# A gated mix of an S4 convolution and linear attention on one core: the written-out issue order, the engine of each step, the PSUM rings and the per-unit forms replaced

## The chip, the cores and the metric

The kernel runs on one core of one Trainium2 chip. The metric is the device time of one execution in microseconds (us); lower is better. The core has five engines that run side by side, each in its own program order: PE (matrix multiply), DVE (vector), ACT (activation functions and copies), POOL (general) and SP (which only issues DMAs here).

## The reference, cut to what matters

Input is one sequence x of 2048 tokens by 512 channels. Two branches are computed from it and mixed by a gate.

```python
g = sigmoid((x * gate_w).sum(-1))
# a: S4 convolution. K[d, l] = Re sum_n C[d,n] * exp(dt*A[d,n]*l) * dt*B[d,n]   (N = 128 states)
#    y = causal convolution of x with K along the tokens (an FFT in the reference), + x * Dskip
# b: linear attention, 32 heads of 16
pq, pk = q @ w_phi, k @ w_phi
phi = concat(softmax(p), softmax(-p))          # for q and for k
kv, z = phi_k^T v, phi_k summed over tokens
o = (phi_q @ kv) / (phi_q @ z + 1e-6);  b = o @ wo
out = g * a + (1 - g) * b
```

Complex exponentials come out as Sin on ACT times Exp on ACT; the softmaxes take Exp on ACT, and their divisions are done as Exp of minus Ln, also on ACT.

## The kernel before, in words

The kernel is built in two passes. First it makes a list of 1058 *nodes*, small steps with a name, an engine, dependencies and a function that issues the step's instructions. Then `Plan.run` goes through the nodes in the order of a string, ORDER (two base-64 digits for a node), and issues each. Since each engine works in program order, the string fixes every engine's sequence; semaphores between engines follow from the dependencies. Further strings fix the rest: SIDES says on which of two engines a step with a choice runs (mostly PSUM evictions, on ACT or DVE), RINGS from which pool of PSUM a step takes its tile, FOURS and ZPS which of two forms some units take. WARM is all zeros.

The steps that matter here, with numbers in the order of their making (`rz#3` is the fourth `rz`):

- Head: `par`, `ld`, `ud`, `wsm`, `wqk`, `wv` are loads on SP's queue; `tgs` (Sin) and `tga` (Abs) make the FFT's tables; `p_e`, `p_d`, `p_g`, `p_ce` (Exp), `p_ab` (Abs) and `p_sn` (Sin) make the tables of the convolution's kernel; `xT` and `udc` bring x into place; `wTe` and `wpe` evict the folded weights.
- FFT of x: matmuls `psAu` and `psBu`, evictions `XAu` and `XU`, 16 each.
- Attention keys, eight pairs of token tiles: `pk` (PE), `ek` (Exp, twice), `zp` (PE) and `zk` (DVE) sum the softmax, `rz` (Ln, then Exp on ACT) inverts the sum, `vp` (PE) and `vb` (eviction) make v, `vr` (DVE) scales it, `kn` (PE) accumulates. ZPS has a digit for each pair: 1 sums groups of four on PE with eight matmuls by the identity and leaves DVE one reduction (L739); 0 lets DVE do it all with two reductions (L736).
- Attention queries, four blocks of 512 tokens: `pq`, `eq` (Exp), `zs`, `z1` (Ln, Exp), `z2`, `z3` (Ln), `z4`, `z5` (Exp), a round trip by DMA, `em`, `ops`, `oT`, `bpsq`, `bs3`. The last block's steps end in L (`eqL`, `z1L`, ...).
- Convolution kernel, 16 units of 32 channels: `argC` (PE) and `cs` (Sin, twice), `argE` (PE) and `E` (Exp), `El`, `Rh`, `Rl`, `A1`, `A2`, `A3` (DVE), `kps` (PE, L183), `KD` (eviction). FOURS has a digit for each unit: 0 adds two products on DVE (`A3`, L1110) and runs 64 matmuls; 1 leaves the add out and runs 128 matmuls.
- FFT of K, product with that of x, and back: `psA`, `XA`, `psB`, `XK`, `t`, `psz`, `Zr` or `Zn`, DMAs `zw` and `zr` through DRAM, `psy`, `ou`, and the output DMAs `out` and `outL` on SP's or ACT's queue. `Y` and `bsg` evict parts of the sum.

ACT holds one table of functions at a time. Nodes `tabT` and `tabL` (the table `natural_log_exp_and_others`) load one explicitly, five times each, through `Tables.begin` (L65); all functions are issued through `Tables.__call__` (L68). Copies and Abs are made from either table. In the list of nodes, each node says which table it wants (`tab=`) and which node sets it (`sets=`), but only the head's Sin and Exp nodes are tied to the table's node by a dependency ("act"), besides the `cs` nodes, which stand in phases between a `tabT` (in the first phase, the end of the head) and a `tabL`; nothing in `run` checks the table.

Of the kernel before, what the change touches and what calls it, by code (L numbers as in the profile page):

```python
# [70 lines left out]
class Plan:  # L71

    DIGITS = "0123456789abcdefghijklmnopqrstuvwxyzABCDEFGHIJKLMNOPQRSTUVWXYZ-_"
    ORDER = ("040B0H0K0d0y0C0D0L0s0I070J0M0P0g000S110j0N08010z0T0m0Q0e2R0a0p0q0r0_0W2T100U0O0V14120Y2U2x0A2S050k130Z2y2V2X2Z0R190v0t0u"
             "0b0c0w2_0l0E0X2W1516172L1a061b2Y022-30311y33340n030f0-"
             "0h1e1f0i1w2J18321c0F0o2B2K2M1n1z1H1g1A1o2D2C1d1p1I091x1E1J351Q1R2F1B0x1C2E0G2H1q36372G2I2P382N2Q391F3b2O3c4C1S3a4J4L4K4M"
             "3d3e4Q4R3f4U1Y3g4N1r4O1h4V3h1L4Y4-"
             "4P3i4Z4_3j4W4S53542z57504T3k4X1Z515b5d58521s1D593l5c3n5i5e55565j3m5a1G3o5q5f5g5s5r5t3p3r3q1T5m5n5u3s5v5h5o5k5w5x5B1P4D4E"
             "3w2v5l5p4F5y5F5C3y1U5H3x5G5I5J5z5A1V5D5E3t3z5U3D5K5V5M5N3A3R3E2w3F5W5L1O5_3G5O5Q5X5Y5Z3B3C1W605R5S1N3K3M1K3S1M5-"
             "5P3L634G642A615T653N673T6869626a666m6n6o3U6p3V3W3X3Y6b6c6q6d6r6s1t3Z3H3-1X3_3O1i1j41401_4221431-"  # L80
             "1k1l204445466e272923222b282d4748243P491m2a4a2c2e4b4g2f4c2g4d252h2o4e4h4i4n1u4j3u3v2j4p2i2l2k2m2q2p6i262s4q4o1v4k2n4u2r2t"
             "6f4v4w6j4r3I2u4x4y4z6g4l8l3J4A8p8m6t6u6k6v8q3Q4f4s6x6h8k8o6l8n8r8s6y6z6w6A6C4m4t4B8C6G8t6I6K8w8x8y8u6B6H6J4H8D8v6L6M6N7d"
             "8z8A8E4I8B7e7f8I7g8F6F9e8Q8G8H9b6O6P8R7h7j7i6Q6R8J9f7M7N8S6S6T6U6Vaeaf7O8W8X8K7k9g8L8T8U8Z8-"
             "938M8N7l6D8_7m8V7n6W6X6Y8O8P8Y7P94an7o7pao7q6_70717r90917Qa47S9295ag7R6Z7s6-"
             "72aha8a9966Ea7akaca5ai73aa75979998ajap7677a69aalatamab74ad7TaBaC7t797u7v7U78au7y7z7V7w7x9caq9naras7AavaH7W9d9h9o9paw7X9v"
             "aY9waK7Y7ZaDaL9q9raZ7a9x9y9zaIc57B7-aM9kc69D9EaQaEbX9L7Cb_aF7D9M7_9Ac07EaRaG9iaxaz80ay9B818285bYaA7Ga-"
             "7IaJ86879j9Fc19s7Jb-"
             "9l9m9Na_7bc7aNaOaPc3cbb2b37HbZc283aS9C7FaT849G9H9I9t89aUaWaV8baX7cccc8c99O9u9P9Q9R888cb87Kb9b0c4caceb19J8abacfcgbg8dck9K"
             "8ecl8f8gbbbh8hbcbibob4cP9Sbpbqcd9T8ichci7L8jcBcCcjcsdYcYctcucycDczdZd-cQcR9Ucmd_cHcvcw9W9Xcnbj9VbwbkblbxcocIbre0eLcp9Ze1"
             "e2b5b6eMbse3eUeVcxb7bye4cqbtbu9Ybdbe9-"  # L90
             "9_cAcrcSbme5cZdOdScEbfcFcGcTcUe6a0a1bve7dTdRdWeNa2e8cJcKe9bzbAedeecLeRcNcOa3eSeaebeOcMc_ePbBd0ecd1d7cVd8d9cWeCdfcXeWdPdU"
             "d2daefege-e_eQd3dbdQdgeTdVd4dndodXdhdcg1g2dieDeEdjeXbKfAbCbnbDbEbFeYfBeZf0f1bGc-dpbLddg7dqbHd5f2drbMf3f4f5bNfGbIbJbOezdk"
             "eAfDdsfEeBeIf6f7feffdldtbPdebQdBfCfHehdueifFejdmf8fgeJd6ekdvfIfJdyf9fafhfbg4fifKg5g6dwfjdzfkfcdxdCdEfLdAdFfMg3g8dGg9dHfN"
             "fleFelfdfmfpdDdLgagbgcgddIeGemeKfqeHfOfPfQfRgeenepfneofreqeresgfggghgifSfTfUfofsbRgjbSgkdJftetglfVfYfZgmgngobUbVgqfufWdM"
             "dNbWgpf-fvfxfygreufwevewexbTeydKfzfXf_g0gvgwgsgtgugx")
    SIDES = ("011111010010101011001110110010011001010100001011100000000000011000011001111101000100000100000000000000000000000010000000"
             "00100001000000000000000101010000000000000100001101001")
    RINGS = ("001010111111010010100000000000000000000000100000000000000000001101100000000101101011100100100001101010111100111001010100"
             "01111")
    WARM = ("000000000000000000000000000000000000000000000000000000000000000000000000000000000000000000000000000000000000000000000000"  # L100
            "000000000000000000000")
    FOURS = ("0111100101011000")
    ZPS = ("01000111")

    HOT = ("pk", "vp", "pq", "zp", "ops", "bps4", "psA", "psBu", "psB128", "psB64", "psB32", "psz", "pszn", "psyn32", "psy128", "psy64", "psy32", "kps")

# [46 lines left out]
    def run(self):  # L153
        code = {d: i for i, d in enumerate(self.DIGITS)}
        order = [64 * code[a] + code[b] for a, b in zip(self.ORDER[0::2], self.ORDER[1::2])] or list(range(len(self.nodes)))
        assert sorted(order) == list(range(len(self.nodes)))
        sides, rings, warm = iter(self.SIDES), iter(self.RINGS), iter(self.WARM)
        for n in self.nodes:
# [501 lines left out]
def attention_keys(P, nc, g, psum, r):  # L660
# [40 lines left out]
    for s2 in range(8):  # L701
# [20 lines left out]

        def ps4(K=K, box=box, on=P.ZPS[s2] == "1"):
            if not on:
                return
            box.ps = bank("zk")
            for u in range(2):
                e = K.E[:, u].rearrange("p g (h a b) -> p (g h) a b", a=4, b=4)
                for k in range(4):
                    nc.tensor.matmul(box.ps[:, 256 * u:256 * u + 256], lhsT=g.ident[:], rhs=e[:, :, k, :], start=(k == 0), stop=(k == 3), skip_group_check=True)  # L730

        def rd(K=K, box=box, on=P.ZPS[s2] == "1"):
            K.Z = g.kwk.tile([128, 2, 2, 32], F32, name="Zk")
            if not on:
                for u in range(2):
                    nc.vector.tensor_reduce(out=K.Z[:, u].rearrange("p g h -> p (g h)"), in_=K.E[:, u].rearrange("p g (h f) -> p (g h) f", f=16),  # L736
                                            axis=mybir.AxisListType.X, op=ALU.add)
                return
            nc.vector.tensor_reduce(out=K.Z[:].rearrange("p u g h -> p (u g h)"), in_=box.ps[:].rearrange("p (z b) -> p z b", b=4), axis=mybir.AxisListType.X, op=ALU.add)  # L739
            box.ps = None  # L740
# [294 lines left out]
def plan_exp(P, nc, g, psum, U, T, psq, deps):  # L1035

    act = g.act
    h, cc = U // 2, U % 2
    box = Bag()

    def pe():
        T.E = g.epool.tile([128, 2, 32, 32], BF16, name="E", bufs=g.P.k["E"])
        box.ps = psum([128, 2, 16, 32], "args")
        for e in range(2):
            nc.tensor.matmul(box.ps[:, e], lhsT=g.statE[64 * e:64 * e + 64, h, :], rhs=g.selE[64 * e:64 * e + 64, 16 * cc:16 * cc + 16, :],
                             start=True, stop=True, tile_position=(64 * e, 0))

    def ex():
        act(out=T.E[:, 1], in_=box.ps[:].rearrange("p e x t -> p (e x) t"), func=ACT.Exp)
        box.ps = None  # L1050

    def el():
        nc.vector.tensor_tensor(out=T.E[:, 0].rearrange("p c (t k) -> p c t k", k=2), in0=T.E[:, 1].rearrange("p c (t k) -> p c t k", k=2),
                                in1=g.G[:, 32 * U:32 * U + 32].unsqueeze(2).to_broadcast([128, 32, 16, 2]), op=ALU.mult)
    a = P.add("PE", "argE", pe, deps, take=[psq, "E"], rw=("stE selE", ""))
    T.nE.append(P.add("ACT", "E", ex, [a], drop=["psum"], tab="L"))
    T.nE.append(P.add("DVE", "El", el, T.nE[-1:], rw=("G", "")))

def plan_conv(P, nc, g, psum, r):  # L1060
# [27 lines left out]
    def kgen(units, XA, new, split=False):  # L1088
        K = Bag()
        K.done, kps, nu = [], [], len(units)  # L1090
        for cc, U in enumerate(units):
            t = T[U]
            plan_exp(P, nc, g, psum, U, t, psq, [sh])
            four = P.FOURS[U] == "1"
            c = Bag()
# [530 lines left out]
```

## Time and profile before

| | us |
|---|---|
| median of 3 runs | 266.88 |
| lowest and highest | 266.54, 267.56 |
| profiled execution, first to last instruction | 265.4 |
| PE busy | 208.8 (79%) |
| PE weight loads busy | 144.6 (54%) |
| DVE busy | 233.9 (88%) |
| ACT busy | 221.7 (84%) |
| POOL busy | 8.4 (3%) |
| mean granted PE clock | 0.933 |

The profile gives the execution's own time as its span alone, 265.4 us; the runs' median is 1.5 us above it. Busy time is the time with an instruction under way; ACT and DVE overlap neighbouring instructions by about a tenth of a microsecond, so a sum of lengths is a little above the time taken. A stage is a stretch of the span, in microseconds from its start.

### The profile page before, as it was taken

The numbers are of one execution on the slowest core, as the hardware profiler recorded it, in microseconds if no ns is written. First come the engines' busy times: TensorE is split into PE (matmuls) and PEld (weight loads), VectorE is DVE, ScalarE is ACT, GpSimd is POOL, SyncE is SP. The second block draws the span as 40 slices with busy tenths as digits, with TensorE's granted clock in tenths as the row PEclk, the third lists the DMA queues.
The fourth block names the chain that finished last, engine by engine and source line by source line (L and its number), as shares of the span: only waits on it lengthen the run. The fifth ranks groups of instructions, "written<-read, shape, count | busy, mean of one in ns | idle before, by whom it ended". The sixth has DMA issues, their size and how long they took to land.

```text
span 265.4 us, 10071 instructions
## 1 busy us (share of the span) xinstructions
PE 208.8 (79%) x4512; PEld 144.6 (54%) x4512; DVE 233.9 (88%) x315; ACT 221.7 (84%) x305; POOL 8.4 (3%) x21
## 2 busy tenths in 40 slices
PE   0768899999964678898857648999997598999760
PEld 0657556655653424447536336775786167965450
DVE  6798898989799989999999999999999798997630
ACT  6989599899899998989999999999999698763300
POOL 4700000000000000000000000000000000000000
PEclk9986799999997579999999999999999799999985
DMA  7799100155510687203243366239753499898776
GB/s 195 130 198 231 23 0 6 63 155 161 145 39 2 195 243 196 84 4 112 73 158 84 100 233 203 76 119 196 160 176 119 167 227 201 207 173 184 161 115 99
DMA packets 67547, 35.93 MB, mean 135 GB/s; under 512 B 46000, under 2 KB 62000, under 8 KB 67504
## 3 DMA queue, kind: packets, MB, share of 16 engines
q1 hardware_dynamic: 65648, 34.76, 53.4%
q8 instruction: 35, 0.57, 1.0%
q10 hardware_dynamic: 1856, 0.52, 1.0%
q14 instruction: 8, 0.07, 0.1%
HBM read 22.17 MB, written 13.11 MB: 133 GB/s over the span
## 4 chain that ended last, share of the span: by engine, by line
PE 39%; DVE 30%; ACT 11%; DMA 9%; issue 7%; SPq 1%; DVEq 0%; ACTq 0%
PE pk L709 6%; PE vp L757 5%; DVE A L1100 4%; DVE R L1121 3%; DVE R L1117 3%; DVE A L1105 3%; DVE Eq L913 3%; PE kps L183 3%; DMA ZT<-Zd 3%; PE psy L824 3%; DMA wqk<-in_B_wqkv_dram 2%; ACT xst L149 2%; DMA ax<-apd 2%; ACT trg L68 2%; PE psA L591 2%
## 5 line engine op out<-in xcount | busy, mean ns | idle before, releaser
L68 ACT ACTIVATE cs<-args 128x1024 bf16<-128x1024 f32 x32 | 30.9, 1052 | 0.9 <-PE args L1023 0.9
L183 PEld LDWEIGHTS <-A 128*32 128x32 bf16 x1536 | 26.4, 161 | 4.8 <-issue 2.0
L183 PE MATMUL kps<-R,A 128*32 128x64 bf16 x1536 | 27.9, 229 | 1.1 <-DVE R L1121 0.7
L1263 PE MATMUL psz<-t,TI 128*128 128x512 bf16 x60 | 16.7, 412 | 5.4 <-DVE t L1231 4.1
L1121 DVE TENSOR_TENSOR R<-E,cs 128x2048 bf16<-128x2048 bf16 x16 | 19.6, 1222 | 0.1
L1105 DVE TENSOR_TENSOR A<-Ctab,Dtab 128x2048 bf16<-128x2048 bf16 x16 | 19.6, 1223 | 0.0
L1100 DVE TENSOR_TENSOR A<-Ctab,Dtab 128x2048 bf16<-128x2048 bf16 x16 | 19.6, 1222 | 0.0
L1117 DVE TENSOR_TENSOR R<-E,cs 128x2048 bf16<-128x2048 bf16 x16 | 19.5, 1220 | 0.0
L149 ACT CAST Zr<-psz 128x1024 bf16<-128x1024 f32 x15 | 15.2, 1022 | 5.1 <-PE psz L1263 3.6
L68 ACT ACTIVATE Ek<-pk 128x512 bf16<-128x512 f32 x32 | 16.7, 601 | 3.2 <-PE pk L709 3.0
L757 PE MATMUL vp<-WW,xT 128*128 128x512 bf16 x64 | 17.8, 419 | 0.0
L1231 DVE TENSOR_TENSOR t<-XUX,XK 128x2048 bf16<-128x2048 bf16 x14 | 16.8, 1222 | 0.4 <-ACT XK L149 0.4
L68 ACT ACTIVATE E<-args 128x1024 bf16<-128x1024 f32 x16 | 16.4, 1036 | 0.6 <-DVE R L1121 0.5
L68 ACT ACTIVATE Eq<-pq 128x512 bf16<-128x512 f32 (+1 forms) x28 | 16.6, 687 | 0.2
L149 ACT CAST XA<-psA 128x1024 bf16<-128x1024 f32 (+1 forms) x15 | 14.6, 1007 | 2.7 <-PE psA L190 2.7
L616 PE MATMUL psB<-XAu,TB 64*128 64x128 bf16 x256 | 11.7, 249 | 6.3 <-ACT XAu L149 3.1
L709 PE MATMUL pk<-WW,xT 128*128 128x512 bf16 x64 | 16.4, 396 | 0.0
L149 ACT CAST XK<-psB 128x1024 bf16<-128x1024 f32 (+1 forms) x14 | 13.7, 990 | 2.5 <-DVE XK L151 1.3
L843 PE MATMUL pq<-xT,Wqp 128*128 128x512 bf16 x64 | 15.5, 380 | 0.2 <-ACT xT L149 0.2
L616 PEld LDWEIGHTS <-TB 64*128 64x128 bf16 x256 | 9.5, 110 | 10.0 <-issue 9.9
L190 PE MATMUL psA<-W,KD 128*64 128x128 bf16 x256 | 9.8, 221 | 5.0 <-ACT cs L68 2.9
L65 ACT ACT_TABLE_LOAD x10 | 12.8, 1283 | 0.1
(211 smaller groups left out, 506.9 us busy)
## 6 DMA issues: line engine op xcount, KB each, us to landing
XUX<-XUd SPq DMA_DIRECT2D x32, 256.0 KB
XUd<-xst SPq DMA_DIRECT2D x8, 512.0 KB
ax<-apd SPq DMA_DIRECT2D x16, 256.0 KB
Zd<-Zr SPq DMA_DIRECT2D x15, 256.0 KB
ZT<-Zd SPq DMA_DIRECT2D x6, 512.0 KB
UD<-in_A_u_dram SPq DMA_DIRECT2D x16, 128.0 KB
XUd<-xst SPq DMA_DIRECT2D x8, 256.0 KB
wqk<-in_B_wqkv_dram SPq DMA_DIRECT2D x1, 1024.0 KB
```

The source lines that it names most:

```text
L68: return self.nc.scalar.activation(**kw)
L149: self.nc.scalar.copy(out=o, in_=i)
L183: nc.tensor.matmul(kps[32 * dj:32 * dj + 32, g4, e, :], lhsT=A[:, ka, :, :, d].rearrange("p a b -> p (a b)"), rhs=R[:, kr, d, :], start=(i ...
L616: nc.tensor.matmul(box.ps[:, c2, sl, :], lhsT=fc.TB[rows, b0:b0 + 2].rearrange("p a b -> p (a b)"), rhs=X.t[rows, k, r0 + sl].rearrange("p ...
L709: nc.tensor.matmul(box.ps[:], lhsT=xT[:, st, kt, :], rhs=g.WW[:, kt, :], start=(kt == 0), stop=(kt == 3))
L757: nc.tensor.matmul(box.ps[:], lhsT=xT[:, st, kt, :], rhs=g.WW[:, 4 + kt, :], start=(kt == 0), stop=(kt == 3))
L1100: nc.vector.tensor_tensor(out=c.A[:, 0:2].rearrange("p o a b c -> p (o a) b c"), in0=g.C[U // 8][:, 0:2, :, d0 % 256:d0 % 256 + 32].rearra ...
L1105: nc.vector.tensor_tensor(out=c.A[:, 2:4].rearrange("p o a b c -> p (o a) b c"), in0=g.C[U // 8][:, 1:3, :, d0 % 256:d0 % 256 + 32].rearra ...
L1117: nc.vector.tensor_tensor(out=c.R[:, :, :, 32:64], in0=t.E[:, 1].unsqueeze(1).to_broadcast([128, 2, 32, 32]), in1=t.cs[:], op=ALU.mult)
L1121: nc.vector.tensor_tensor(out=c.R[:, :, :, 0:32], in0=t.E[:, 0].unsqueeze(1).to_broadcast([128, 2, 32, 32]), in1=t.cs[:, ::-1, :, ::-1], o ...
L1231: nc.vector.tensor_tensor(out=box.t, in0=Ls[r0 // ns].X[:], in1=box.XK[:].unsqueeze(1).to_broadcast([128, 2, 1024]), op=ALU.mult)
L1263: nc.tensor.matmul(box.ps[:, hb, :], lhsT=fc.TI[:, k].rearrange("p t h a -> p (t h a)"), rhs=box.t[:, k, 512 * hb:512 * hb + 512], start=( ...
```

## The change

The strings ORDER, SIDES, RINGS, FOURS and ZPS are replaced. The list of nodes, their functions and their dependencies are the same. SIDES moves 48 steps to the other engine; FOURS goes from 8 to 12 units without the add, ZPS from 4 to 8 pairs summed on PE.

```diff
@@ class Plan
-    ORDER = ("040B0H0K0d0y0C0D0L0s0I070J0M0P0g000S110j0N08010z0T0m0Q0e2R0a0p0q0r0_0W2T100U0O0V14120Y2U2x0A2S050k130Z2y2V2X2Z0R190v0t0u"
...
+    ORDER = ("0H0K0I0J0M0S0B0C0D190y0z0A0m0n0o0d0e0f0g0h0i0102031d0j0k0l000T0p0q0r0405060s0t0u0708090L110a0b0c2R0_2T0P0Q2B0N122D100U0W"
...
-    SIDES = ("011111010010101011001110110010011001010100001011100000000000011000011001111101000100000100000000000000000000000010000000"
-             "00100001000000000000000101010000000000000100001101001")
-    RINGS = ("001010111111010010100000000000000000000000100000000000000000001101100000000101101011100100100001101010111100111001010100"
-             "01111")
+    SIDES = ("111111101101110000000000011111111001000000001101100100010010010000010011110000000000000011010000000001000000000000000000"
+             "00000000000000000000001100010100000000100010001001001")
+    RINGS = ("101010110100110000000000000000000000000001100000000000000000011111000000101110001000011011101010101111100100110010000001"
+             "00111")
...
-    FOURS = ("0111100101011000")
-    ZPS = ("01000111")
+    FOURS = ("1111111111101000")
+    ZPS = ("11111111")
```

Read off the strings, ACT's sequence of the nodes that need a table, with the table nodes in brackets. It begins at the second `tabT`; steps that need no table are left out.

Before:

```
[tabT#1] p_sn#1 p_sn#0 p_sn#2 p_sn#3 p_sn#4 p_sn#5 p_sn#6 p_sn#7 cs#1 cs#2 cs#0 cs#3
[tabL#1] E#0 eq#0 eq#1 E#1 eq#2 eq#3 eq#4 eq#5 z1#0 E#2 eq#6 z3#0 eq#8 z5#0 E#4 eq#7 E#3 z1#1 eq#9 z3#1 E#5 z5#1 eq#10
[tabT#2] cs#4 cs#7 cs#5 cs#6  [tabL#2] eq#11 E#6 z1#2 z3#2 z5#2 E#7 E#8
[tabT#3] cs#8 cs#9 cs#11 cs#10  [tabL#3] E#9 E#11 E#10 eqL#0 eqL#1 z1L#0 E#12 z3L#0 E#13 z5L#0
[tabT#4] cs#12 cs#15 cs#13 cs#14  [tabL#4] E#15 E#14
```

After:

```
[tabT#1] p_sn#0 rz#0 p_sn#1 p_sn#2 rz#1 g_e#0 ek#4 p_sn#3 ek#5 ek#6 rz#2 ek#7 p_sn#4 rz#3 ek#8 p_sn#5 ek#9 p_sn#6 p_sn#7
         rz#4 ek#10 ek#11 ek#12 ek#13 rz#5 cs#1 rz#6 cs#3 cs#0 E#0 E#1 ek#14 ek#15 cs#2 eq#4
[tabL#1] E#2 eq#0 rz#7
[tabT#2] eq#2 eq#1 cs#4 eq#3 E#4 E#3 eq#8 z1#0 cs#6 eq#6 z3#0 E#5 eq#5 z5#0 cs#5 eq#7 eq#9 z1#1 E#6 cs#7 z3#1
[tabL#2] eq#10 z5#1 eq#11  [tabT#3] cs#8 z1#2 E#7 z3#2 z5#2 cs#11 E#8 cs#9 E#9 E#10 cs#10 eqL#0 eqL#1 E#11 z1L#0 z3L#0
[tabL#3] z5L#0 E#12  [tabT#4] cs#12 E#13 cs#13 cs#15 cs#14 E#15 E#14  [tabL#4]
```

More of the change, by code (lines that the diff above doesn't have):

```diff
@@ L73 @@
     DIGITS = "0123456789abcdefghijklmnopqrstuvwxyzABCDEFGHIJKLMNOPQRSTUVWXYZ-_"
-    ORDER = ("040B0H0K0d0y0C0D0L0s0I070J0M0P0g000S110j0N08010z0T0m0Q0e2R0a0p0q0r0_0W2T100U0O0V14120Y2U2x0A2S050k130Z2y2V2X2Z0R190v0t0u"
[L75 to L95, printed above, removed]
@@ L96 @@
-    SIDES = ("011111010010101011001110110010011001010100001011100000000000011000011001111101000100000100000000000000000000000010000000"
-             "00100001000000000000000101010000000000000100001101001")
-    RINGS = ("001010111111010010100000000000000000000000100000000000000000001101100000000101101011100100100001101010111100111001010100"
-             "01111")
+    ORDER = ("0H0K0I0J0M0S0B0C0D190y0z0A0m0n0o0d0e0f0g0h0i0102031d0j0k0l000T0p0q0r0405060s0t0u0708090L110a0b0c2R0_2T0P0Q2B0N122D100U0W"
+             "0O130V0Y0R142S2x2y2U0X0Z2V15160-172X0v0w0x18352C1a1b1y2Z2W2E1c1H1e1n2-1f1o2_2Y30361w1p1I1Q1z2F2G1L1g1O1q1r1s1A31322L2H37"
+             "0E0F0G1K2M1J1x331P1R1B1E1C342P381F2I1S2N2Q2O2J392K1N4C1D3b4Y3c3a4J1G1Y4Z3d1h1i1j3f3g3e1T4L4Q4K4M3h4-1U4R3i3j3l4N3k1V1M2A"
+             "3m1W3n4U3o4_504V1X3p4O3r1Z533q1-3s3t3u3v3R27204P3w3x4W514D4E3y1_293z5254573D5q3F283E5b3S4S4T4X2158553A3B3C3T4F2b4H223G3H"
+             "3I3J595d563U5a5c2a5e3K4I2c243L3M3N5r5f5i5g5j5h3V3X2d3W2e5m5n5s5t3Z3Y3-5k5x5y5o3_5u405v23415l5p432f2o5w5F42442h5H5B5G5z2g"
+             "5I2i45475C482p5D25462q5M5J5Q5K2j493O3P3Q5N4b5U4a2r5A1k1l1m1t1u1v5E2k4g5R5W4c4i5L2s5S5O4d4e4f674j2l5P5V4h2v2w5T2t264n4p4k"
+             "4l4m2m695X5Y5Z684o4q4u4w6a6b2n2u4v6c4x4r4s4t8l5-4y4z4A4B5_608p638n646e61656d6i8k626f6j6g8w6k6m8r8o8t8C8u8v8D6o666t8z6n6u"
+             "7d8x8m8A6p6G6q8q8I7e8y8Q8E8B6r6x8J8s8F8R8S6H8G6s8Wa46Ia86h6K6l8H2z6v6y6z8X6L8K6J6w6A6M8L8Taea96N6B7f8Zaf8U8-937M8_7N8M8N"
+             "8V8Oag6F6O7ha68P8Y6P6Qab947i7j906Ran6Sao917g6T6C6D6Ea5aaak7O6U6V6W9h9i9japal7k92957QaBah96977P98at7l7maCa7acaiajam7n6X6Y"
+             "6Z7o6-73ad9974au9aaq9e9f9g7R7p7S75ar6_70717q727T4GaDbXasaHavb_77aw9b9c9d7r7s7t7U799nc0aE9oaFaI9v9w7u7v7waK9p9x7V7W9qaGaL"
+             "9r9y9D7x789z7y7z7A9E7X7YaQb2b3b47a9L9M7Zax9k9l9mb-7C7E7B7-7_80ayc3aM9F768182837DaJaNaRc5c67G7I7Jaz8586879A9B9CaOc7aYaZa-"
+             "7FaA849N7bbY7Hc188cb7caPaSceaT89cfc87K8baU8a8caVaWaX8d8e8f9s9t9u7L9G9H8gb8b9ckcccgbaa_b0b18h8i8jbgcsc9bhca9O9P9I9J9Kclbi"
+             "bodYbZctcucdbpd-chcic2dZd_9Q9R9Sbbcj9T9U9VcVcWcXbccB9W9X9YcCcmcnbwbjcPcQcRcye0bqczbxbke1cocqcvcwb5b6b7cpcHcxe2crcAcDe3eL"
+             "c4blbmbncEe4cFbdbebf9ZcI9-e5cGeMdOa0a19_cJe6e7e8brbye9eaebdSeOdTcKcLedeeefbscMbtbubvcNcScTcUcOc_bzeNd0bAbBbCbDePa2eRd1d7"
+             "ecd2ega3d8d9dfeQd3dRcYcZc-eUdnd4d5d6bEbFbGeVdadgdPeFeGeHeSdodUdbeTdhdidjeWdcdddedpdWdQe-bHbIbJe_dVeXdkdldmeYbKdqdreZbLds"
+             "dtdug1g2f0f1fDfAfBbNbOf2bMf3f4ezeAeBeheifGbPfCfEdBf5eCeDeEfFf6fef7fHbQfff8fIf9fJdvdwdxfgfadydzdAdCeIeJeKfhg3g7dDfig4g8fK"
+             "ejfLfjfkflekdEdFdGg5g6dHfMfNelg9fOfbfcfdgagbfPfQbUbVbWgcfRdIdJdKgdgefmfnfofpfqfrepgfeqerfSfTfUbRbSbTemfseneogggighgjgkdL"
+             "dMdNftfVfWfXfYfZf-esewexeyglgmgngogpf_eteuevfxfyfzg0fufvfwgqdXgrgsgtgugvgwgx")
```

## The prediction

> **What bounds the kernel now.** I read the page first for the shares, then busy time by stage, then the ACT rows of the timeline, because the new order moves instructions on ACT across the points where its function table is changed. Busy time first: one line of the page, then the stages I cut (their columns: length, then busy us of each engine, granted clock, DMA share, GB/s).
>
> ```profile
> PE 208.8 (79%) x4512; PEld 144.6 (54%) x4512; DVE 233.9 (88%) x315; ACT 221.7 (84%) x305; POOL 8.4 (3%) x21
> ```
> ```profile
> 30.00:75.00 45.00, 44.34 (x762) 27.00 (x761) 38.93 (x53) 39.36 (x78) 0.00 (x0) 0.98 0.29 82
> 75.00:105.00 30.00, 20.13 (x302) 11.85 (x302) 28.98 (x50) 29.03 (x31) 0.00 (x0) 0.77 0.47 133
> 105.00:145.00 40.00, 32.69 (x881) 21.30 (x881) 39.76 (x50) 38.71 (x59) 0.00 (x0) 1.00 0.29 94
> 145.00:185.00 40.00, 31.75 (x630) 22.65 (x631) 39.97 (x42) 39.65 (x51) 0.00 (x0) 1.00 0.55 151
> 185.00:222.00 37.00, 31.37 (x843) 23.36 (x837) 34.83 (x36) 32.60 (x38) 0.00 (x0) 0.95 0.66 168
> 222.00:266.00 44.00, 31.40 (x952) 23.48 (x951) 27.51 (x33) 16.76 (x23) 0.00 (x0) 0.90 0.81 161
> ```
>
> To be seen: from 75 to 185 us DVE and ACT are both full (97 to 100%), from 30 to 75 PE is. From 30 to 222 us ACT works 179.35 of 192 us, so it has 12.65 us to spare there. Only after 222 us is it half idle. Now the groups of ACT that change its table, and the timeline around three of the loads (start, length, what).
>
> ```profile
> L65 ACT ACT_TABLE_LOAD x10 | 12.8, 1283 | 0.1
> ```
> ```profile
> 0.73 1.28 ACT L238 ACT_TABLE_LOAD   x1 [0.73 <-PEq L1610]
> 2.02 0.20 ACT L238 CAST if<-ii 128x8 f32<-128x8 int32 x1
> 2.24 1.28 ACT L65 ACT_TABLE_LOAD   x1
> ```
> ```profile
> 105.27 1.28 ACT L65 ACT_TABLE_LOAD   x1
> 106.56 1.02 ACT L68 ACTIVATE E<-args 128x1024 bf16<-128x1024 f32 x1
> 107.48 1.08 ACT L68 ACTIVATE Eq<-pq 128x512 bf16<-128x512 f32 x2
> ```
>
> To be seen: ten loads are the steps tabT and tabL of the program (L65). One more carries the line of a plain CAST (L238): nobody wrote it, so the builder puts a load ahead of an instruction whose table isn't known to be in place. It did so although the next ACT step, 0.22 us behind that CAST, loads another table anyway: it looks at the one instruction and not ahead. The load also ran before the CAST's operand was there, so it doesn't wait itself.
>
> **The table loads, the main term.** In the order of before, all Sin steps (tgs, p_sn, cs) lie between a tabT and the next tabL, and all Exp and Ln steps (p_d, p_ce, ek, rz, E, eq, z1, z3, z5) between a tabL and the next tabT; I read ACT's sequence off the string and find no exception, which agrees with eleven loads in the profile. In the new string I find them mixed: behind tabT#1 come p_sn#0, rz#0, p_sn#1, p_sn#2, rz#1, ek#4, p_sn#3, ek#5 and so on; later cs#3, cs#0, E#0, ek#14, cs#2, eq#4; cs#6, eq#6; cs#9, E#9; cs#10, eqL#0; cs#12, E#13, cs#13. Following the active table along that sequence, it changes from Sin to Exp or Ln without a written load 20 times, and back to Sin 16 times: 36 loads that the builder must add, if one table holds Exp and Ln together. The kernel gets that table by its name, natural_log_exp_and_others. Where the builder picks by the one function ahead, it may take one that has Exp alone, and another that has Ln alone; then Ln behind such an Exp (8 times), and Exp behind such an Ln (13 times, inside every rz and z1 but rz#7 and behind two z3), load as well: 57. I take 57, since L238 shows a choice without looking ahead; 36 is a rival. The ten written loads stay, useful or not; the last, tabL#4, now stands behind all the arithmetic, between two output DMAs. So 56 more lie ahead of unit 14's E, the last Exp.
>
> Price of one: 1.283 us (L65). Where it parts two independent instructions it also takes their overlap: E at 106.56 lasts 1.02 us and the next starts 0.92 us on, 0.10 us of overlap; with the 0.02 us gaps on the load's sides about 1.41 us. Between Ln and Exp of one rz the two don't overlap (73.30 + 0.31, next at 73.64), so 1.28 us. 43 x 1.41 + 13 x 1.28 = 77.3 us; lower bound 56 x 1.28 = 71.7.
>
> The Trainium skill (ScalarE: Activation LUTs, What ACT_TABLE_LOAD costs) puts a switch at about 2.66 us, 1.283 for the load and 1.38 for a drain. The trace agrees with the first half; it has no drain between the load's neighbours, 0.02 us ahead and 0.01 behind. An estimate by that page: 56 loads would be 149 us, and the sum below 405.
>
> **What ACT gains or loses otherwise.** Sides that flip, by the rows of their groups: XAu -4 x 1.04, udc -3 x 1.04, xT -2 x 1.0, KD -1.03, Zr -1.01, XA +1.04, XK +1.6, vb +3 x 0.6, oT +0.6, wTe and wpe +1.0 each: -4.3 us of length, -3.9 as spacing.
>
> **DVE.** FOURS goes from 8 to 12 units: four adds fewer (L1110), -4.9. ZPS from 4 to 8: two L736 reductions of 1.21 become one L739 of 0.69, four times, -6.9. selE goes to POOL, -1.2 (there about 3, from the 1.50 us of half its size, L473; its reader is PE's first args, 35 us later in before; diagD queues behind it and is read later still). Sides: XAu +4.9, udc +1.3, xT +1.4, KD +1.2, Zr +1.2, vb -2.1, XK -1.9, XA -1.2, wpe -1.2, oT and wTe -1.4. Together about -10.8 of 233.9.
>
> **PE.** Four units with 128 instead of 64 kps matmuls: 256 x 27.9/1536 = 4.7 us. Four more zp groups of 0.92 us in the chain: 3.7. All 8.4 us hide behind ACT, which grows by far more in every stage. Without that cover the 3.7 would count in full: PE is at 44.34 of 45 us there.
>
> **Queues.** On SP, wqk is now first; it landed at 7.88 us and released PE, so the head gains at most the 0.5 us of Bim's issue. Small reads after that shift by issue times of about 0.5 us; their readers sit behind ACT. The xup, zw and zr issues keep their place relative to the steps that they follow. At the end the ACT queue issues outL#1 ahead of Zn#1, which is in the chain: four issues took 6.33 us, so up to 3.2 us for its two, and up to 1.3 us for tabL#4 ahead of out#7. Against that, DVE and PE reach the tail with their queues worked off: up to -4. I take 0, from -4 to +3.
>
> **The sum.** From the profiled execution, 265.4 us: +77.3 loads, -3.9 flipped sides, less what of the loads falls into ACT's 12.65 us of idle time between 30 and 222 us (7 taken: a load need not wait, but the PE round trips early on stay), tail 0: 331.8. The runs' median lies 1.5 us above that span, so 333. DVE's gain isn't in the sum: with ACT behind, nobody waits for DVE. The last E, at 220.86 in before, should start near 288.
>
> Bounds: low, 71.7 and not 77.3, all 12.65 us covered, tail -4: 316.5, as time 318. High: no idle covered and tail +3, 342; and the order's own waits unseen, with ACT as idle everywhere as in its worst stages (5.6 of 45, 4.4 of 37, about 12%): 253 us of ACT work between 30 us and the last E would take 287, some 22 more idle than now, span 361. Nothing asks for the worst share in all stages, so I stop at 352; I widen the low end to 314 for a few loads that I may have miscounted.
>
> **Rivals.** *36 loads*: the builder takes a table with both Exp and Ln. 35 x 1.41 = 49.4; 265.4 + 49.4 - 3.9 - 7 + 1.5 = 305. For it: the kernel has that table in use. Against: the choice at L238. The Trainium skill (ScalarE: Activation LUTs, Table sets) gives ln then exp as one load, since a set with both exists; by that rule it would be this rival, and no run so far shows what is picked.
> *Faster, no extra loads*: were mixed steps served by the table at hand, ACT would lose 3.9 us and DVE, which is full from 75 to 185 us, 4.9 of adds there and some flipped sides, about -7: 260. It decides as long as fewer than about 10 loads are added (7 us gained and 7 of idle, at 1.4). Against: L238 and L65, which would be there for nothing.
> *Waits dearer*: rings of one (A, KD) and two (E, kps) tie DVE and PE to a late ACT and ACT to them in turn; over 352, toward 361.
>
> **Chances.** Forecast 0.84, 36 loads 0.08, faster 0.04, dearer waits 0.04. The range of the forecast, 314 to 352, leaves out the other three and no more than 0.2 with its own edges. A measurement here tells about 0.5% (1.3 us) from no change; every case but one is slower by more, and of that one I leave a quarter to a gain too small to tell.
>
> **What would show it.** ACT_TABLE_LOAD about 68 times, most under L68, each 1.28 us; ACT busy near 291 us and 97% or more from 30 to 290 us; DVE and PE both under 75%; DVE and PE waits put down to ACT. Wrong, if loads are near 11 (then nothing of this holds), near 47 (305), or ACT has long idle times in the middle.

## The result: 328.2 us against 266.7, 23% slower

The new kernel takes 328.22 us (median of 4 runs, 325.93 to 328.64), the old one 266.71 beside it (265.17 to 267.56). The ratio is 1.230, with a 95% interval of 1.224 to 1.237. The profiled execution's own time is 327.92 us, its span 326.0. Medians are over all executions, ratios over those in the faster of two states that some kernels show.

The page of the new kernel, busy time:

```profile
PE 224.2 (69%) x4778; PEld 153.7 (47%) x4800; DVE 226.4 (69%) x308; ACT 292.1 (90%) x360; POOL 12.1 (4%) x22
```

ACT went from 221.7 to 292.1 us, DVE from 233.9 to 226.4. Stages of the new kernel (length, then busy us of PE, PEld, DVE, ACT, POOL, granted clock, DMA share, GB/s):

```profile
30.00:60.00 30.00, 23.88 (x413) 15.47 (x415) 22.20 (x39) 29.77 (x41) 0.00 (x0) 0.89 0.28 81
60.00:90.00 30.00, 21.59 (x265) 13.19 (x269) 20.50 (x31) 29.77 (x38) 0.00 (x0) 0.89 0.17 45
90.00:140.00 50.00, 33.17 (x689) 17.96 (x695) 31.69 (x39) 48.32 (x63) 0.00 (x0) 0.90 0.26 76
140.00:200.00 60.00, 36.43 (x821) 23.09 (x821) 34.54 (x47) 58.91 (x72) 0.00 (x0) 0.78 0.28 83
200.00:240.00 40.00, 29.92 (x743) 22.90 (x744) 30.48 (x31) 39.80 (x47) 0.00 (x0) 0.97 0.49 119
240.00:285.00 45.00, 33.76 (x792) 24.86 (x795) 33.83 (x34) 41.39 (x45) 0.00 (x0) 0.87 0.65 163
```

From 30 to 285 us ACT is busy 248 of 255 us. PE and DVE, which were full in the old kernel from 30 to 75 and from 75 to 185 us, are now at 58 to 80%. The three groups of table loads, by line:

```profile
L68 ACT ACT_TABLE_LOAD x57 | 73.1, 1283 | 1.4 <-PE zs L863 0.4
...
L65 ACT ACT_TABLE_LOAD x10 | 12.8, 1283 | 1.0 <-issue 0.8
...
L234 ACT ACT_TABLE_LOAD x1 | 1.3, 1283 | 0.7 <-PEq L1606 0.7
```

57 loads that nobody wrote stand under the line of the function calls, beside the eleven of before. The timeline of ACT where the first of them come, behind the second written Sin load (`trg` is written by p_sn, `Zk` and `vr` by the Ln and the Exp of rz, `xst` by XU):

```profile
40.70 1.28 ACT L68 ACT_TABLE_LOAD   x1
42.00 0.31 ACT L68 ACTIVATE Zk<-Zk 128x128 f32<-128x128 f32 x1
42.33 1.28 ACT L68 ACT_TABLE_LOAD   x1
43.62 0.31 ACT L68 ACTIVATE vr<-Zk 128x128 bf16<-128x128 f32 x1
43.84 0.99 ACT L145 CAST xst<-psB 128x1024 bf16<-128x1024 f32 x1
44.85 1.28 ACT L68 ACT_TABLE_LOAD   x1
46.14 2.01 ACT L68 ACTIVATE trg<-pb 128x1024 bf16<-128x1024 f32 x2
48.16 1.28 ACT L68 ACT_TABLE_LOAD   x1
49.46 0.31 ACT L68 ACTIVATE Zk<-Zk 128x128 f32<-128x128 f32 x1
```

One rz, 0.62 us of work, brings three loads: one for Ln, one for Exp, one back to Sin. And the waits of the new kernel, those of DVE and PE among the longest (engine and line, what it waited for, us in total, times, longest):

```profile
DVE den L874 <- ACT den L68: 14.6, 4, 4.9
DVE vr L762 <- ACT vr L68: 11.2, 5, 5.1
DVE A L1096 <- PE kps L179: 10.9, 7, 2.6
PE args L1041 <- ACT cs L68: 10.7, 6, 4.8
...
PE args L1019 <- ACT E L68: 7.3, 2, 5.8
DVE E L1049 <- ACT E L68: 6.9, 3, 5.0
```

All but one of these wait for ACT, at Sin, Exp and Ln steps, which are those that a load can stand beside. Summed over all lines of the view, DVE waits 61.3 us for ACT against 5.4 in the old kernel, PE 65.1 against 26.0.

**Where the time went, in one sum.** I split ACT's time from the span's start to the start of the last E into the head (0.73 us in every run), loads, other instructions (by their spacing, so that an overlap isn't counted twice) and idle time, and call the rest of the span the tail. Loads are counted up to that E; us; from the traces:

| kernel | loads | their us | other work | idle | last E starts | tail | span |
|---|---|---|---|---|---|---|---|
| before | 11 | 14.1 | 189.7 | 16.4 | 220.9 | 44.6 | 265.4 |
| after | 67 | 86.0 | 188.4 | 9.7 | 284.8 | 41.3 | 326.0 |
| e1 | 46 | 59.0 | 187.7 | 11.4 | 258.9 | 39.6 | 298.5 |
| e2 | 3 | 3.8 | 185.4 | 28.7 | 218.7 | 42.0 | 260.6 |
| e3 | 3 | 3.8 | 190.3 | 23.5 | 218.4 | 46.0 | 264.4 |
| e5 | 67 | 86.0 | 188.8 | 10.5 | 285.9 | 39.7 | 325.6 |
| e6 | 33 | 42.3 | 189.5 | 7.5 | 240.0 | 44.8 | 284.8 |
| r1 | 11 | 14.1 | 188.5 | 59.1 | 262.4 | 39.4 | 301.7 |

Before to after: loads +71.9, other work -1.2, idle -6.7, tail -3.3: +60.6 us, which is the difference of the spans. Each trace is one execution: the first pk matmul stands at 30.1 us in the old kernel's and at 27.9 in e8's, though nothing ahead of it was changed, so 1 or 2 us between two of these rows can be the execution's and not the kernel's.

### The profile page after: what moved, and what is told of

Read it like the earlier page. It is cut to its first block, busy times and chain, and to the rows that moved or that the text cites. A ratio compares the mean times of both kernels' runs of the same rounds, so it can differ in the third digit from the quotient of the medians.

```text
span 326.0 us, 10666 instructions
## 1 busy us (share of the span) xinstructions
PE 224.2 (69%) x4778; PEld 153.7 (47%) x4800; DVE 226.4 (69%) x308; ACT 292.1 (90%) x360; POOL 12.1 (4%) x22
## 5 line engine op out<-in xcount | busy, mean ns | idle before, releaser
L179 PE MATMUL kps<-R,A 128*32 128x64 bf16 x1792 | 32.0, 235 | 8.4 <-ACT E L68 3.9
L179 PEld LDWEIGHTS <-A 128*32 128x32 bf16 x1792 | 30.5, 160 | 12.4 <-issue 9.8
L68 ACT ACTIVATE cs<-args 128x1024 bf16<-128x1024 f32 x32 | 30.8, 1025 | 0.1
L762 DVE TENSOR_TENSOR vr<-vb,vr 128x1024 bf16<-128x1024 bf16 x16 | 10.8, 688 | 15.1 <-ACT vr L68 11.2
L753 PE MATMUL vp<-WW,xT 128*128 128x512 bf16 x59 | 19.2, 451 | 1.2 <-issue 0.7
L68 ACT ACTIVATE Ek<-pk 128x512 bf16<-128x512 f32 x32 | 17.6, 630 | 0.0
L839 PE MATMUL pq<-xT,Wqp 128*128 128x512 bf16 x64 | 17.1, 396 | 0.3 <-ACT Ek L68 0.3
L145 ACT CAST XA<-psA 128x1024 bf16<-128x1024 f32 (+1 forms) x16 | 15.6, 1008 | 1.7 <-PE psA L186 1.7
L68 ACT ACTIVATE Eq<-pq 128x512 bf16<-128x512 f32 (+1 forms) x28 | 16.8, 670 | 0.1
L145 ACT CAST XK<-psB 128x1024 bf16<-128x1024 f32 (+1 forms) x16 | 15.5, 994 | 1.5 <-PE psB L192 1.5
L68 ACT ACTIVATE E<-args 128x1024 bf16<-128x1024 f32 x16 | 16.3, 1035 | 0.1
L1041 PE MATMUL args<-selE,statE 64*128 64x512 bf16 x32 | 7.1, 436 | 13.2 <-ACT cs L68 10.7
L1049 DVE TENSOR_TENSOR E<-E,Gtab 128x1024 bf16<-128x1024 bf16 x16 | 10.8, 682 | 6.9 <-ACT E L68 6.9
```

Of the source, the lines that this page charges most:

```text
L68: return self.nc.scalar.activation(**kw)
L145: self.nc.scalar.copy(out=o, in_=i)
L179: nc.tensor.matmul(kps[32 * dj:32 * dj + 32, g4, e, :], lhsT=A[:, ka, :, :, d].rearrange("p a b -> p (a b)"), rhs=R[:, kr, d, :], start=(i ...
L753: nc.tensor.matmul(box.ps[:], lhsT=xT[:, st, kt, :], rhs=g.WW[:, 4 + kt, :], start=(kt == 0), stop=(kt == 3))
L839: nc.tensor.matmul(box.ps[:, m - m0, :] if late else box.ps[:], lhsT=g.Wqp[:, kt, 128 * m:128 * m + 128], rhs=xT[:, 4 * b:4 * b + 4, kt, : ...
```

## The experiments

The theory was that the added loads are all of the loss, since ACT is the bound from 30 us to the last E. The rivals: the order, the sides or the forms cost by themselves; the loads hide in waits; a load is dearer than its length.

**e1, the joint table by name.** Fewer loads, the same order of the work:

```diff
-        done = set()
+        done, self.tab = set(), None
...
+            if n.at == "ACT":
+                if n.sets:
+                    self.tab = n.sets
+                elif n.tab == "L" and self.tab != "L":
+                    self.nc.scalar.preload_act_table_set(LN_EXP)
+                    self.tab = "L"
+                elif n.tab == "T" or n.name == "p_sn":
+                    self.tab = "T"
             n.fn()
```

> The new order, with the joint Ln and Exp table loaded by its name ahead of the first such step behind a Sin step. Ln behind Exp and Exp behind Ln then need no load: 47 table loads instead of 68. Theory (ACT is the bound from 30 us to the last E, a load costs what it takes there, 1.3 us): 21 x 1.3 = 27 us less than the 328.2 of the new kernel, 301. Rival (the new order is bad by itself, its loads fall largely into waits): 5 to 10 us less, 318 to 323.

Measured: 300.9 us (300.25 to 303.62). Its loads:

```profile
L172 ACT ACT_TABLE_LOAD x20 | 25.7, 1283 | 0.4
...
L68 ACT ACT_TABLE_LOAD x16 | 20.5, 1283 | 0.3
...
L65 ACT ACT_TABLE_LOAD x10 | 12.8, 1283 | 1.0 <-issue 0.8
...
L242 ACT ACT_TABLE_LOAD x1 | 1.3, 1283 | 0.7 <-PEq L1614 0.7
```

20 named, 16 back to Sin, as counted off the string. 21 loads fewer are worth 27.3 us, 1.30 each: the theory's number, and against a loss in the order itself, the rival's 318 to 323. It also shows that the builder's own choice of tables, one for Exp and one for Ln, was 27 of the 61 us lost.

**e2 and e3, one table.** Both orders, freed of nearly all loads:

```diff
-    trg = P.add("ACT", "tabT", lambda: act.begin(TRIG), rw=("", "act"), sets="T")
+    trg = P.add("ACT", "tabT", lambda: None, rw=("", "act"), sets="T")
...
-        S("p_sn", lambda: act(out=F.sc[:, 0], in_=X(), func=ACT.Sin, scale=TURN), r="act B0", w="s0")
+        S("p_sn", lambda: act(out=F.sc[:, 0], in_=X(), func=ACT.Exp, scale=TURN), r="act B0", w="s0")
```

The other Sin of p_sn, the two of cs, and the table nodes of the phases are changed in the same way. Both kernels leave out the sines behind the head and so don't compute the reference's result; the instructions' shapes stay.

> The new strings, but the Sin of p_sn and cs is computed as Exp (their values are not those of the reference) and the eight written loads behind the head are left out: 3 table loads remain, all else is as in the new kernel. Theory (the loads are all of the loss): 65 loads fewer and ACT no longer the only bound; DVE's 226 us of work and about 35 us of head and tail give 250 to 262, below the one-table form of the old order by what DVE saves, 2 to 8 us. Rival (the order, the sides or the rings cost by themselves): above the old order's one-table form by 5 us or more.

> The old strings with the same change of Sin to Exp and without the eight written loads behind the head: 3 loads instead of 11. It is the base for the new strings without loads. Theory: 8 x 1.3 = 10 us of ACT work less, but DVE is as full as ACT from 75 to 185 us, so 3 to 8 us less than 266.7: 259 to 264. Rival (ACT alone sets the pace of the old order): the full 10 us, 256.

Measured: e2 262.54 us (261.53 to 263.82), ratio to the old kernel 0.988 (0.981 to 0.995); e3 266.51 (263.8 to 269.53), ratio 1.000 (0.995 to 1.005). So without loads the new strings are not worse than the old ones but, by the medians, 4.0 us better, and the loads are all of the loss; e2 lies half a microsecond above the upper edge of its theory. How much of these 4.0 us is the strings' own is open: e2's runs had a granted clock of 0.944 to 0.970, e3's 0.911 to 0.938, and the old kernel's own runs beside the experiments go from 264.2 us at 0.950 to 268.1 at 0.915. Of e3 both expectations missed: eight loads fewer, 10.3 us of ACT work, gained nothing that can be told. Its stages from 75 to 145 us:

```profile
75.00:105.00 30.00, 20.59 (x309) 12.88 (x307) 29.59 (x52) 28.49 (x32) 0.00 (x0) 0.77 0.49 144
105.00:145.00 40.00, 32.14 (x937) 21.64 (x935) 39.80 (x48) 35.46 (x57) 0.00 (x0) 1.00 0.26 85
```

DVE is busy 99% there and ACT now 91%: ACT's idle time up to the last E grew from 16.4 to 23.5 us, and of the 2.5 us by which the last E came forward a tail 1.5 us longer took most. In the old order DVE sets the pace there, and the eight loads cost nothing that these runs can tell. One thing beside DVE plays in: from 140 to 155 us DVE's steps come 1.5 us early in e3's trace, and at 156.5 us, behind a wait of 0.84 us for PE, 0.6 us are left; the granted clock from 145 to 165 us was 0.66 in e3 and 1.00 in the old kernel. About 0.9 us of the missing gain may be the clock's.

**e6, the price of a load where nothing else moves.** The old kernel with loads of the table that is active anyway:

```diff
+            if n.name in ('E', 'rz'):
+                self.nc.scalar.preload_act_table_set(LN_EXP)
             n.fn()
```

> The old strings, with one more load of the table that is active anyway ahead of each of the 16 E steps and 8 rz steps: 35 loads instead of 11, order and work unchanged. It prices a load where nothing else moves. Theory (ACT full, 1.3 us each, less some idle time in the stage where PE is the bound): 24 x 1.3 = 31 less about 5, so 290 to 296. Rival (a load hides in the waits of ACT): below 275. Rival (a load drains the engine and costs 2.7 us): 325 or more.

Measured: 287.32 us (285.62 to 288.32). The trace has 22 added loads, not 24:

```profile
L173 ACT ACT_TABLE_LOAD x22 | 28.2, 1283 | 0.4
```

(Ahead of E#0 and E#15 the trace has only the written load of the same table, at 109.17 and 235.49 us.) 20.5 us for 22 loads, 0.93 each, below the 290 to 296 of the theory: two loads fewer, and they take 28.2 us on ACT, of which 8.9, not 5, fell into its idle time (16.4 to 7.5 us in the table). So eight loads cost nothing that can be told where DVE is full (e3), a load costs 0.9 us in an order in which ACT has idle time left to cover it (e6; and 38.4 us for the 44 loads between e2 and e1, 0.87 each), and 1.3 where its idle time hardly shrinks any more (from e1 to the new kernel, 11.4 to 9.7 us). The rival of 2.7 us is out. The loads of e6 don't change the table; those between e1 and the new kernel do, and at 1.30 us each they cost hardly more than their length of 1.28.

**e5, the new order with the old forms.** Does DVE's saving count?

```diff
-    FOURS = ("1111111111101000")
-    ZPS = ("11111111")
+    FOURS = ("0111100101011000")
+    ZPS = ("01000111")
```

> The new order, sides and rings with the old FOURS and ZPS: DVE gets 11.8 us of work back, PE loses 8.4; 68 table loads as in the new kernel. Theory (with ACT behind, nobody waits for DVE): the same as the new kernel's 328.2 within 3 us. Rival (DVE's saving was part of the 328): 334 to 340.

Measured: 327.45 us (327.37 to 328.44), as the theory has it: DVE is busy 237.1 us and not 226.4, and the 10.7 us more change nothing.

**e4, e7 and e8, the new forms in the old order**, both together, FOURS alone, ZPS alone:

```diff
-    FOURS = ("0111100101011000")
-    ZPS = ("01000111")
+    FOURS = ("1111111111101000")
+    ZPS = ("11111111")
```

> The old order, sides and rings with the new FOURS and ZPS: four adds and four pairs of DVE reductions fewer (4.9 and 6.9 us of DVE work), 256 kps matmuls and 32 zp matmuls more on PE; 11 table loads. Theory (DVE and ACT are both full from 75 to 185 us, PE from 30 to 75): a small gain from the adds, at most 4.9, against up to 3.7 lost on PE early on: 262 to 268. Rival (DVE alone was the bound there): 257 to 262. Rival (the extra matmuls of kps delay KD and the chain behind it): 268 to 272.

> The old strings with only the new FOURS: four adds of 1.22 us fewer on DVE, 256 kps matmuls more on PE. With both new forms the old order lost 9.4 us (266.7 to 276.1), 3.7 of them ahead of the first E in the profiles. Theory (each form stretches a step on PE that the order was laid out around; a unit without the add has twice the matmuls in the chain from the products to KD): 4 to 6 us slower, 271 to 273. Rival (the loss came from the sums of the keys alone): 262 to 267.

> The old strings with only the new ZPS: four pairs of DVE reductions become four groups of eight matmuls and one reduction; DVE loses 6.9 us of work, PE gains 3.7 in the stage where it is full. Theory (PE sets that stage, DVE has room in it): 3.5 to 5 us slower, 270 to 272. Rival (DVE's saving is worth as much as PE's loss): 265 to 268.

Measured: e4 276.14 us, ratio 1.036 (1.030 to 1.041); e7 271.57, ratio 1.020 (1.015 to 1.026); e8 270.13, ratio 1.012 (1.006 to 1.018). Of e4 none of the three expectations held, the theory of a small gain least: less DVE work made the old order slower, by the ratio 9.5 us. By their ratios FOURS makes 5.3 of it and ZPS 3.2, as the theories of e7 and e8 have it. ZPS first; stage 30 to 75 us of e8, and DVE's longest wait:

```profile
30.00:75.00 45.00, 44.21 (x774) 27.68 (x773) 29.02 (x46) 37.08 (x71) 0.00 (x0) 1.00 0.28 80
```
```profile
DVE Zk L739 <- PE zk L730: 8.6, 7, 2.2
```

PE was full there and still is; DVE went from 38.9 to 29.0 us and waits for PE. From the first pk matmul to the last rz it is 48.1 us in e8's trace (27.9 to 76.0) and 44.1 in the old kernel's (30.1 to 74.2): 4.0 more, beside the 3.7 us of added sums. For FOURS, DVE's longest wait in e7 is one that is not among the longest of the old kernel (its list begins at 2.4 us):

```profile
DVE A L1100 <- PE kps L183: 4.8, 4, 3.1
```

With 128 matmuls PE reads the one buffer of A for longer, and DVE waits to write the next unit's products. That is in part argued: from the first cs to the last E it is 128.7 us in e7's trace and 124.1 in the old kernel's, DVE is idle 8.3 us more of it, and this wait is 4.8 of them; the others are smaller waits for PE and ACT.

**r1 and r2, the Sin steps grouped again.** ORDER of the new kernel with only such moves that each table is loaded by a written load (r1), or with the early Sin steps in two groups (r2); the rest of the order follows the new one as far as dependencies and buffers let it.

```diff
-             "3m1W3n4U3o4_504V1X3p4O3r1Z533q1-3s3t3u3v3R27204P...
...
+             "3m1W3n4U3o4_504V3p4O3r1Z533q3s3t3u3v3R4P3w3x4W51...
...
```

This is the start of the changed part of r1's string. r2 has its own string and, as e1 does, the code that loads the joint table by name: 15 loads.

> The new sides, rings and forms, and the new order with only the moves that bring all Sin steps back between a written Sin load and the next written load of the joint table, as in the old order: 11 table loads, nothing else changed in what is computed. Theory (the loads are all of the loss): near the 262.5 of the one-table form of the new order, plus what the moves disturb, 262 to 272. Rival (the order lives from the mixing; grouping pushes the Sin steps of the kernel's tables behind all keys and DVE idles before): 275 to 285.

> As r1, but the eight Sin steps of the kernel's tables stay early, in two groups of four between the attention keys, with the joint table loaded by name behind each group: 15 table loads. Theory (ACT has room for some loads while DVE is the bound): 260 to 268, below r1, since DVE gets its table work early. Rival (each load counts at 1.3 us): r1 plus 5 us.

Measured: r1 304.38 us (302.73 to 306.62), r2 302.78 (299.3 to 306.84). No expectation of either was near, and with 11 loads r1 is slower than e1 with 47. The waits of r1 say why:

```profile
PE args L1019 <- ACT cs L68: 28.0, 5, 18.4
DVE A L1096 <- PE kps L179: 10.1, 6, 2.0
DVE R L1113 <- ACT cs L68: 9.7, 3, 5.9
```

PE's next args sit in a queue and wait for PSUM that a cs step, held back for its group, has yet to read (18.4 us at the longest), and ACT is idle for 59 us. These two say that my grouping is bad, not that every grouping is. No kernel with the whole computation in it beat the old one; e2's 262.5 us is what the new strings would give if the tables cost nothing.

## Why the prediction was right, point by point

- *57 loads, not 36.* Right to the load: 57 under L68, 68 in all. The choice by the one function ahead, read off L238, held; which table the builder picks for an Exp no run had shown, so there the prediction was also lucky. The Trainium skill (ScalarE: Activation LUTs, Table sets) counts ln then exp as one load; here the builder put two, at 40.70 and 42.33. Where the joint table was named (e1), it is one. That rival was priced at 305, and e1 measured 300.9.
- *Price of a load.* 1.283 us of its own, as before, and no drain: at 48.16 a load ends where the next instruction starts 0.02 us later. The Trainium skill (ScalarE: Activation LUTs, What ACT_TABLE_LOAD costs) has 2.66 us for a switch; this trace doesn't agree.
- *Lost overlap, 5.5 us.* The overlap itself came out: up to the last E, neighbours on ACT overlap by 29.1 us in sum in e2 and by 23.9 in the new kernel, the same instructions with 64 loads more. One place where a load stands in the new kernel, at 48.16, as it is in e2:

```profile
42.22 2.00 ACT L68 ACTIVATE trg<-pb 128x1024 bf16<-128x1024 f32 x2
44.12 0.30 ACT L68 ACTIVATE Zk<-Zk 128x128 f32<-128x128 f32 x1
```

  The second starts 0.10 us before the first ends. What the sum had not: the instructions became shorter, from 214.5 to 212.3 us in sum, most of it (1.7) at those beside a load. So other work rose by only 3.0 us, from 185.4 to 188.4, 0.047 us a load and not 0.10.
- *Flipped sides, -3.9 us.* From e3 to e2, both with three loads, other work falls by 4.9. Together with the 3.0 above, by the table: -1.2 us measured where the sum had +1.6, 2.8 us of the 5.8 by which the span came out below the 331.8 of the sum.
- *Idle time covered, 7 us.* Measured 6.7 (16.4 to 9.7).
- *Tail, 0 from -4 to +3.* Measured -3.3, the other part of the error. e2, in which ACT isn't behind, already has -2.6, so most of it comes with the new strings and not with DVE and PE waiting. The feared ACT queue cost nothing: outL#1's two issues took 0.88 us, and Zn#1 behind them waited for DVE:

```profile
313.74 0.88 ACTq L991 DMA_DIRECT2D out_dram<-xT  x2
...
314.56 0.69 DVE L147 CAST Z<-psz 128x512 bf16<-128x512 f32 x1 [0.90 <-PE psz L1293]
...
315.29 0.58 ACT L145 CAST Z<-psz 128x512 bf16<-128x512 f32 x1 [4.13 <-DVE Z L147]
```

- *Last E near 288.* It started at 284.8, for the reasons above.
- *DVE's gain isn't in the sum.* e5: 327.45 against 328.22. Its own size was a little off, 7.5 us (233.9 to 226.4) where the list had 10.8.
- *PE's 3.7 us count in full without ACT's cover.* e8, without it: 1.2%, 3.2 us. For FOURS the prediction named no such price, 4.7 us of matmuls "behind ACT"; without the cover it was 5.3 (e7).
- *Faster without loads, 260.* e2: 262.5, so the gain is 4 us, not 7, and by the clocks perhaps less. The part that failed is the worth of the forms: in the old order they cost and don't gain (e4), so the new strings must make up for that elsewhere, or suit the forms; which of the two was not tried.
- *Signs.* ACT busy 292 us (near 291 expected), 97.2% of 30 to 285 us and 96.8% of 30 to 290; PE and DVE at 69%.

## What to carry to other kernels

Before an issue order is changed, follow the state that the order carries along, here ACT's function table, through the new sequence and count its changes: an operation that "stays the same" can bring another with it that nobody wrote. Name a table that serves the whole mix instead of leaving the choice to a step at a time, which alone was 27 us here. And an engine's saved work is worth nothing, or less, where it is not the one waited for: the forms that spare DVE some 11 us changed nothing behind a full ACT, and cost the old order 9.5 us, where they add to PE's work (208.8 to 215.5 us busy in e4).

## What was not expected

The new kernel's granted clock is lower though PE works less: 0.891 as a mean against 0.933, and 0.78 from 140 to 200 us with PE busy 36 of 60 us. In that stretch it goes with PE's work in the kernels of the new order: 0.76 with PE busy 35 us (e5), 0.91 with 43 (e1), 0.97 with 49 (e2). What sets it was not tried.
